# One chain of row maxima per attention head instead of four, and new numbers for the scheduler of a fused attention and MLP kernel

## The chip, the cores and the metric

The kernel runs on one core of one Trainium2 chip. A core has TensorE (PE, matrix products; its weight loads are shown apart as PEld), VectorE (DVE), ScalarE (ACT), GpSimd (POOL) and SyncE (SP, which here issues nearly all DMAs). The matmuls write to PSUM, 8 banks of 128 x 512 float32 values. The metric is the time of one execution on the device in microseconds (us), the median of several runs; lower is better.

## What is computed

The input x is 2048 x 1024 and is normalised row by row. Two branches read the result: an attention with 32 heads of width 32, and an MLP of width 3584 with the mish activation. The output is x + s * silu(mlp).

```python
qkv = (xn @ wqkv).reshape(B, S, 3, H, Dh)            # S 2048, H 32, Dh 32
scores = jnp.einsum("bhqd,bhkd->bhqk", q, k) * (Dh ** -0.5)
p = _softmax(scores, axis=-1)
o = jnp.einsum("bhqk,bhkd->bhqd", p, v)
s = o.transpose(...).reshape(B, S, D) @ wo
h = jnp.einsum("bsd,df->bsf", xn, w1) + b1           # F 3584
act = h * jnp.tanh(softplus(h))
g = _silu(jnp.einsum("bsf,fd->bsd", act, w2))
return x + s * g
```

## The kernel before

Matrix values that need full precision are split into a high and a low part (fp32r), and a product is made of three matmuls: high x high, high x low, low x high.

The work has three stages. First come the norm, the projections to q, k and v, and the splitting of the MLP's weights; their results go to DRAM. The second stage runs attention and MLP together, and its order is made by a planner (class `Plan`, L78) while the program is built. The third stage is the rest of the output projection with the gate (`op` matmuls, L1107).

In the second stage five streams offer matmuls to the planner, and every other operation is an `Op` (L67) with an engine, a duration, needs, and rings from which it takes a place (PSUM banks and SBUF tiles).

- `s_stream` (L684) makes the scores of head h a first time, only for their maxima. For each of 16 query tiles (`qt`) and 4 key chunks (`kc`) one 128 x 512 matmul `s` (L695) goes to a bank, and VectorE reduces the bank to one column of maxima (`mx`, L701).
- `m_chain` (L711) turns maxima into something that a matmul can use. Its steps: the maximum over the 4 chunks, negated (`nm`, DVE L714); high and low part (`hl`, a copy on ACT and a subtraction on POOL); a transpose on PE (`mtp`, L527); a copy to SBUF (`mt`, ACT); and two DMAs on SP's queue that write rows 96 and 97 of the head's q stack. Before, it runs once for each group of 4 query tiles, four times a head.
- `t_stream` (L761) makes the scores again, transposed, with the negated maxima already added by rows 96 and 97: for key tile T (16 a head) four matmuls `t` (L775), each followed by an exponential on ACT (`p`, L264). POOL adds up the tiles `p` into `z` (L804, one add per tile), and after 6, 5 and 5 key tiles (`GROUPS`, L32) `product` (L814) issues the matmuls `pv` (L822). `norm` (L838) makes the sums with the matmuls `zp` (L848) and divides on DVE (L859, L862, L865).
- `h_stream` (L909) and `y_stream` (L996) make the MLP: 24 matmuls `h` (L923) per tile, mish on DVE and ACT (L942 to L978), and the matmuls `y` (L1011), whose results DVE adds up in `yacc` (L1031).
- `p_stream` (L1110) begins the output projection.

The q and k stacks of a head lie in one of three pairs of SBUF tiles. `stack_load` (L681) loads the pair of head h with six DMAs of 256 KB, after the last `t` of head h-3. SP issues in the planner's order, and each DMA waits there for what it needs, so that a waiting one holds back those behind it. Weight tiles `w1` (1 MB) and `w2` (512 KB) and a head's `v` go through the same queue.

The planner goes forward in its own time. At each step it takes, for the engine that is free first, the ready operation with the smallest key. For the matmuls of the streams the key is a due time: for `s` it is that of the `t` in `LEAD` key tiles before the next head's first one. For the others it is the time at which they became ready, less `urgent`: a negative `U_MX` holds the maxima back behind others. `S_B`, `T_B` and `D_B` are the banks that `s`, `t` (with `mtp`) and the MLP (with `zp`) may hold at one time, of seven in all; `LATE` delays `mtp` and `zp` unless PE is already in the products' column mode; `Y0` is the lag of `y` behind `h`.

Of the kernel before, what the change touches and what calls it, by code (L numbers as in the profile page):

```python
# [9 lines left out]
F32 = mybir.dt.float32  # L10
F32R = mybir.dt.float32r
AF = mybir.ActivationFunctionType
ALU = mybir.AluOpType
AX = mybir.AxisListType
# [4 lines left out]
P = 128  # L19
KT = D // P  # L20
NC = S // 512
NT = S // P
# [4 lines left out]
W1_V = 20  # L27
NS = H * NT

MM, PV = 0.228, 0.86  # L30

GROUPS, YB = (6, 5, 5), 2  # L32

LEAD, LATE = 5, 4.0

PS, ACTS, W2S, Y0, Y1 = 7, 3, 5, 0.6, 0.17

AHEAD, BEHIND = 1.5, 1

S_B, T_B, D_B = 2, 2, 4  # L40

U_MX, U_Y = -2.0, 1.0


class Later:
# [32 lines left out]
class Plan:  # L78
# [7 lines left out]
    SETTLE = 0.2  # L86

    AHEAD = {"DVE": 0.08, "ACT": 0.1, "POOL": 0.0}
    SEM, SWITCH, LAND, RATE = 0.07, (0.25, 0.13), 2.0, 0.25e6

    def __init__(self):
        self.at = {"PE": 0.0, "ACT": 0.0, "DVE": 0.0, "POOL": 0.0, "SP": 0.0}
# [122 lines left out]
def body(ctx: ExitStack, tc: tile.TileContext, x, wqkv, wo, w1, b1, w2, out):  # L215
    nc = tc.nc
# [6 lines left out]
    def pool(stack, name, bufs, side="left", **kw):  # L223
        return stack.enter_context(tc.tile_pool(name=name, bufs=bufs, side=side, reuse_waits="tile", **kw))
# [41 lines left out]
    def copy(out_, in_, scale=1.0):  # L266
        nc.scalar.activation(out_, in_, AF.Copy, scale=scale)  # L267

    def move(out_, in_, eng=None):

        (eng or nc.sync).dma_start(out_.bitcast(F32), in_.bitcast(F32))

    def low(eng, out_, in_, high):

        eng.tensor_tensor(out_, in_, high.bitcast(F32), ALU.subtract)  # L275
# [137 lines left out]
    for t in range(2, NT + 2):  # L413
# [19 lines left out]
        if t > 7:  # L433
            c, k = t // 4 - 1, t % 4 * 2
# [63 lines left out]
    early = pool(att0, "early", 1, side="right")  # L498
    qst, kst = [], []
# [16 lines left out]
    hls = [early.tile([P, P], F32R, name=f"hl{i}") for i in range(2)]  # L516
# [6 lines left out]
    def parts(i):  # L523
        return hls[i][:, :8].rearrange("p (a b) -> p a b", a=2)

    def turn(tp, i):
        nc.tensor.matmul(tp[:, :P], hls[i], ident_r, start=True, stop=True)  # L527
# [141 lines left out]
    def bank(at, name):  # L669
        return ps_a.tile([P, 512], F32, tag=f"b{at['b']}", name=name)  # L670

    def op(*args, **kw):
        return plan.add(Op(*args, **kw))

    total = 2 * 4 * NS * MM + NC * FT * 48 * MM + NS * PV
    slot = total / NS


    loaded, m_there, last_t, last_pv, final, stored = {}, {}, {}, {}, {}, {}
# [5 lines left out]
    def s_stream():  # L685
        for h in range(1, H):
            while h not in loaded:
                yield None
            for g in range(4):
                maxes, tiles = [], {}  # L690
                for qt in range(4 * g, 4 * g + 4):
                    for kc in range(4):
                        def mm(at, h=h, qt=qt, kc=kc, tiles=tiles):
                            tiles[qt, kc] = sp_ = bank(at, f"s{h}_{qt}_{kc}")
                            nc.tensor.matmul(sp_, qst[h % 3][:, qt * P:(qt + 1) * P],  # L695
                                             kst[h % 3][:, kc * 512:(kc + 1) * 512], start=True, stop=True)

                        def mx(at, h=h, g=g, qt=qt, kc=kc, tiles=tiles):
                            if qt == 4 * g and kc == 0:
                                tiles["mx"] = early.tile([P, 4, 4], F32, tag=f"mx{at['mx']}", name=f"mx{h}_{g}")  # L700
                            nc.vector.reduce_max(tiles["mx"][:, qt % 4, kc:kc + 1], tiles[qt, kc], axis=AX.X)  # L701

                        m = Op("PE", MM, key=slot * (16 * (h - 1) + qt + (kc + 1) / 4 - LEAD), need=[loaded[h]],
                               emit=mm, take=["s", "b"])
                        yield m
                        maxes.append(op("DVE", 0.69, need=[m] + maxes[:1], emit=mx, give=[("s", m), ("b", m)], urgent=U_MX,
                                        take=["mx"] if qt == 4 * g and kc == 0 else []))
                m_chain(h, g, maxes, tiles)
        final["s"] = m

    def m_chain(h, g, maxes, tiles):  # L711
        def r1(at):
            tiles["nm"] = early.tile([P, 4], F32, tag=f"nm{at['nm']}", name=f"nm{h}_{g}")
            nc.vector.tensor_reduce(tiles["nm"], tiles["mx"], axis=AX.X, op=ALU.max, negate=True)  # L714

        def r2(at):
            tiles["hl"] = at["hl"]
            copy(parts(tiles["hl"])[:, 0], tiles["nm"])

        def r3(at):  # L720
            hl = parts(tiles["hl"])
            low(nc.vector if h == 0 else nc.gpsimd, hl[:, 1], tiles["nm"], hl[:, 0])

        def r4(at):
            tiles["tp"] = tp = bank(at, f"mtp{h}_{g}")
            turn(tp, tiles["hl"])

        def r5(at):
            tiles["mt"] = early.tile([8, P], F32R, tag=f"mt{at['mt']}", name=f"mt{h}_{g}")
            copy(tiles["mt"], tiles["tp"][:8, :P])  # L730

        def r6(at):
            for a in range(2):
                move(qst[h % 3][96 + a:97 + a, g * 512:(g + 1) * 512]
                     .rearrange("o (t p) -> o t p", p=P), tiles["mt"][4 * a:4 * a + 4, :])

        a = op("DVE", 0.18, need=maxes, emit=r1, take=["nm"], give=["mx"])
        a = op("ACT", 0.21, need=[a], emit=r2, take=["hl"])
        a = op("POOL" if h else "DVE", 0.25, need=[a], emit=r3, give=["nm"], key=-1)
        a = op("PE", 0.07, need=[a], emit=r4, take=["t", "b"], give=["hl"], late=LATE if h else 0.0)  # L740
        a = op("ACT", 0.28, need=[a], emit=r5, take=["mt"], give=[("t", a), ("b", a)])
        m_there[h, g] = op("SP", 0.2, need=[a], emit=r6, give=["mt"], bytes_=4096)


    exps, adds, uses = {}, {}, {}
# [415 lines left out]
    plan.take_now("mx", 1)  # L1161
    loaded[1] = None
    m_chain(0, 3, [], {"mx": negm[0]})
    plan.run([t_stream(), s_stream(), h_stream(), y_stream(), p_stream()])
    ph.close()

# [46 lines left out]
    for c in range(NC):  # L1213
        for s in range(4):
            t = 4 * c + s
            if t + 4 < NT:
                start(t + 4)
            for dh in range(2):
# [5 lines left out]
                if c:  # L1224
                    n = 2 * s + dh
# [39 lines left out]
```

## Time and profile before

| what | before |
|---|---|
| median of 3 runs | 3448.2 us |
| lowest and highest run | 3447.49 and 3449.71 us |
| profiled execution: span from first to last instruction | 3445.5 us |
| profiled execution: own total beside the span | not given |
| granted TensorE clock, mean | 1.000 |
| busy: PE, PEld, DVE, ACT, POOL | 99, 74, 68, 57, 72% of the span |
| the planned stage, first `s` of head 1 to first `op` | 578.65 to 3267.09 us |

Times in rows are in us from the span's start unless they are marked ns. A row of a group has line, engine, operation, out<-in, shapes and count, then busy us and mean ns of one, then the engine's idle time before them and what ended it. A row of the timeline has start, duration, engine, line, operation and count, and in brackets the idle time before it with its releaser. L12 is line 12 of the kernel. Matmuls overlap in these rows: one starts before the last has ended, so that a row's duration is not the time from one to the next.

### The profile page before, as it was taken

To read this page: it belongs to the slowest core of one execution; us is meant where nothing else is said; L and a number is where in the kernel's file an instruction comes from. 1 tells how busy PE (TensorE), PEld (TensorE's weight loads), DVE (VectorE), ACT (ScalarE), POOL (GpSimd) and SP (SyncE) were. 2 spreads that over 40 slices of the span, in tenths; PEclk is the share of its full clock that TensorE was granted. 3 is DMA by queue.
4 is the path that set the end of the run, shared out by engine and by line. 5 is a ranking of instruction groups with operands and counts; after the bars stand their busy time and mean duration, and the time that the engine had idled before them with its cause. 6 is when DMAs were issued, how large, how long until landed. Compare 5 with 4: busy or idle time off the path is not lost.

```text
span 3445.5 us, 48527 instructions
## 1 busy us (share of the span) xinstructions
PE 3414.9 (99%) x17920; PEld 2546.2 (74%) x17920; DVE 2341.4 (68%) x3843; ACT 1962.8 (57%) x3298; POOL 2469.8 (72%) x846
## 2 busy tenths in 40 slices
PE   8999999999999999999999999999999999999999
PEld 8998887676777767777667677677777777776787
DVE  6012236887878777787788778778877787776633
ACT  6111112666666667666666676666666666666621
POOL 0644342898888888888888888888888888888800
PEclk9999999999999999999999999999999999999999
DMA  8998896443434354343433443334345444334382
GB/s 293 299 298 303 288 319 223 112 120 99 118 105 122 105 165 134 113 117 104 123 111 111 147 144 115 111 102 119 111 122 160 135 122 122 108 103 132 119 309 86
DMA packets 294193, 529.80 MB, mean 154 GB/s; under 512 B 88810, under 2 KB 147178, under 8 KB 270186
## 3 DMA queue, kind: packets, MB, share of 16 engines
q1 hardware_dynamic: 274100, 484.74, 45.6%
q10 hardware_dynamic: 19856, 41.95, 3.4%
q8 instruction: 142, 2.33, 0.3%
q14 instruction: 95, 0.78, 0.1%
HBM read 386.89 MB, written 138.67 MB: 153 GB/s over the span
## 4 chain that ended last, share of the span: by engine, by line
PE 95%; DVE 2%; ACT 2%; issue 1%; DMA 1%; POOL 1%; SPq 0%; POOLq 0%; ACTq 0%
PE h L923 17%; PE y L1011 17%; PE pv L822 13%; PE t L775 13%; PE s L695 13%; PE qk L623 10%; PE op L1107 5%; PE v L324 5%; ACT p L264 1%; DVE mx L701 1%; PE zp L848 1%; PE s L550 0%; POOL z L804 0%; DMA qstack<-mt 0%; PE mtp L527 0%
## 5 line engine op out<-in xcount | busy, mean ns | idle before, releaser
L804 POOL TENSOR_TENSOR z<-z,p 128x2048 f32<-128x2048 f32 x448 | 2065.8, 4611 | 195.8 <-ACT p L264 173.2
L264 ACT ACTIVATE p<-t,zero 128x512 f32<-128x512 f32 x2048 | 1376.7, 689 | 625.2 <-PE t L775 615.6
L701 DVE TENSOR_REDUCE mx<-s 128x1 f32<-128x512 f32 x1984 | 1323.0, 685 | 454.1 <-PE s L695 450.4
L1011 PE MATMUL y<-w,act 128*128 128x512 f32 x2688 | 928.0, 392 | 1.0 <-DVE yacc L1031 0.8
L775 PE MATMUL t<-qstack,kstack 128*128 128x512 f32 x2048 | 799.0, 394 | 5.3 <-DMA qstack<-mt 3.0
L695 PE MATMUL s<-kstack,qstack 128*128 128x512 f32 x1984 | 777.6, 395 | 6.3 <-DVE mx L701 3.2
L923 PE MATMUL h<-xr,w 128*128 128x512 f32 x2016 | 693.9, 391 | 1.0 <-ACT p L264 1.0
L1011 PEld LDWEIGHTS y<-w,act 128*128 128x128 f32 x2688 | 502.0, 188 | 114.9 <-issue 4.2
L775 PEld LDWEIGHTS t<-qstack,kstack 128*128 128x128 f32 x2048 | 384.4, 188 | 124.7 <-issue 25.4
L695 PEld LDWEIGHTS s<-kstack,qstack 128*128 128x128 f32 x1984 | 371.3, 188 | 119.6 <-issue 18.4
L822 PE MATMUL pv<-p,v 128*32 128x512 f32 x4096 | 459.3, 594 | 0.0
L923 PEld LDWEIGHTS h<-xr,w 128*128 128x128 f32 x2016 | 376.8, 188 | 84.6 <-issue 3.4
L623 PE MATMUL qk<-xc,qkw 128*128 128x512 f32 x1536 | 350.9, 389 | 0.0
L804 POOL TENSOR_TENSOR z<-p,p 128x2048 f32<-128x2048 f32 x32 | 147.9, 4621 | 278.6 <-ACT p L264 218.7
L623 PEld LDWEIGHTS qk<-xc,qkw 128*128 128x128 f32 x1536 | 288.2, 188 | 59.8
L822 PEld LDWEIGHTS pv<-p,v 128*32 128x32 f32 x4096 | 123.3, 110 | 281.5 <-issue 281.1
L1031 DVE TENSOR_TENSOR yacc<-yacc,y 128x512 f32<-128x512 f32 x416 | 282.7, 680 | 47.4 <-PE y L1011 45.2
L923 PE MATMUL h<-xc,w 128*128 128x512 f32 x672 | 233.3, 391 | 0.4 <-DVE yacc L1031 0.4
L275 DVE TENSOR_TENSOR qst<-qk,qst 128x512 fp32r<-128x512 f32 x64 | 44.2, 691 | 246.2 <-ACT qst L267 246.2
L267 ACT ACTIVATE qst<-qk 128x512 fp32r<-128x512 f32 x64 | 38.3, 598 | 302.6 <-PE qk L623 287.4
L324 PE MATMUL v<-vw,xc 128*128 128x256 f32 x1536 | 190.8, 285 | 2.9 <-POOL vw L275 1.5
L324 PEld LDWEIGHTS v<-vw,xc 128*128 128x128 f32 x1536 | 186.6, 193 | 4.5 <-POOL vw L275 1.9
(91 smaller groups left out, 2391.2 us busy)
## 6 DMA issues: line engine op xcount, KB each, us to landing
w<-w1s SPq DMA_DIRECT2D x112, 1024.0 KB
w<-w2s SPq DMA_DIRECT2D x224, 512.0 KB
w2s<-pw SPq DMA_DIRECT2D x56, 512.0 KB
qstack<-qs SPq DMA_DIRECT2D x96, 256.0 KB
kstack<-ks SPq DMA_DIRECT2D x96, 256.0 KB
w1s<-w1p SPq DMA_DIRECT2D x20, 1024.0 KB
praw<-in_B_w_dram SPq DMA_DIRECT2D x72, 256.0 KB
x<-in_A_x_dram SPq DMA_DIRECT2D x32, 512.0 KB
```

The source lines that it names most:

```text
L264: nc.scalar.activation(out_, in_, fn, bias=zero if bias is None else bias, scale=scale)
L324: nc.tensor.matmul(ps[:, :256], xc[t // 4][:, a, k, (t % 4) * P:(t % 4 + 1) * P], w[:, b, k], start=n == 0, stop=n == 3 * KT - 1)
L623: nc.tensor.matmul(ps, w[:, a, k], xc[c][:, b, k], start=n == 0, stop=n == 3 * KT - 1)
L695: nc.tensor.matmul(sp_, qst[h % 3][:, qt * P:(qt + 1) * P], kst[h % 3][:, kc * 512:(kc + 1) * 512], start=True, stop=True)
L701: nc.vector.reduce_max(tiles["mx"][:, qt % 4, kc:kc + 1], tiles[qt, kc], axis=AX.X)
L775: nc.tensor.matmul(tp, kst[h % 3][:, kt * P:(kt + 1) * P], qst[h % 3][:, c * 512:(c + 1) * 512], start=True, stop=True)
L804: nc.gpsimd.tensor_tensor(zs[h], pts[T - 1] if kt == 1 else zs[h], pts[T], ALU.add)
L822: nc.tensor.matmul(pv[h][c * DH:(c + 1) * DH, :], vt[h][:, k, :], pts[T - kt + k][:, c * 512:(c + 1) * 512], start=k == 0, stop=k == NT - 1)
L923: nc.tensor.matmul(t["h"], w1t[n][:, a, k], xts_[c][:, b, k], start=i == 0, stop=i == 3 * KT - 1)
L1011: nc.tensor.matmul(t["y"], acts[n][:, p, s * P:(s + 1) * P], w2t[m_][:, q], start=j == 0 and i == 0, stop=j == YB - 1 and i == 2)
L1031: nc.vector.tensor_tensor(ya, ya, t["y"], ALU.add)
L1107: nc.tensor.matmul(ps[t, dh], ohl[t // 4, k][:, a, s * P:(s + 1) * P], wt[k][:, b, r], start=k == 0 and i == 0, stop=k == KT - 1 and i == 2)
```

## The change

There are two parts. `s_stream` no longer makes groups: the maxima of a whole head go to one tile of 16 x 4 columns, and `m_chain` runs once a head with n = 16 query tiles. Its tiles have 16 and 32 columns or rows instead of 4 and 8, and its two DMAs write 2048 columns instead of 512. The part of head 0 that the planner does still runs with n = 4. Head h's first `t` now needs the only chain of its head, so the maxima of all 16 query tiles.

The other part is the table of numbers for the planner.

```diff
-MM, PV = 0.228, 0.86
+MM, PV = 0.22667, 0.8587
-LEAD, LATE = 5, 4.0
-
-PS, ACTS, W2S, Y0, Y1 = 7, 3, 5, 0.6, 0.17
+LEAD, LATE = 15, 3.0
+
+PS, ACTS, W2S, Y0, Y1 = 7, 3, 5, 1.2, 0.17
-S_B, T_B, D_B = 2, 2, 4
-
-U_MX, U_Y = -2.0, 1.0
+S_B, T_B, D_B = 2, 2, 5
+
+U_MX, U_Y = 0.0, 1.0
...
-    SEM, SWITCH, LAND, RATE = 0.07, (0.25, 0.13), 2.0, 0.25e6
+    SEM, SWITCH, LAND, RATE = 0.07, (0.2, 0.125), 2.0, 0.25e6
...
-            for g in range(4):
-                maxes, tiles = [], {}
-                for qt in range(4 * g, 4 * g + 4):
-                    for kc in range(4):
+            maxes, tiles = [], {}
+            for qt in range(NT):
+                for kc in range(4):
...
-                m_chain(h, g, maxes, tiles)
+            m_chain(h, 0, maxes, tiles, NT)
...
-    def m_chain(h, g, maxes, tiles):
+    def m_chain(h, g, maxes, tiles, n=4):
+        kind = "mh" if n == NT else "m"
+
+        def hl_parts():
+            return hls[tiles["hl"]][:, :2 * n].rearrange("p (a b) -> p a b", a=2)
...
-            tiles["mt"] = early.tile([8, P], F32R, tag=f"mt{at['mt']}", name=f"mt{h}_{g}")
-            copy(tiles["mt"], tiles["tp"][:8, :P])
+            tiles["mt"] = early.tile([2 * n, P], F32R, tag=f"{kind}t{at['mt']}", name=f"mt{h}_{g}")
+            copy(tiles["mt"], tiles["tp"][:2 * n, :P])
...
-        a = op("PE", 0.07, need=[a], emit=r4, take=["t", "b"], give=["hl"], late=LATE if h else 0.0)
+        a = op("PE", 0.12, need=[a], emit=r4, take=["t", "b"], give=["hl"], late=LATE if h else 0.0)
...
-        m_there[h, g] = op("SP", 0.2, need=[a], emit=r6, give=["mt"], bytes_=4096)
+        a = op("SP", 0.2, need=[a], emit=r6, give=["mt"], bytes_=1024 * n)
+        for c in range(g, g + n // 4):
+            m_there[h, c] = a
```

The order changes everywhere in the second stage. Three places show how. In the names, s14_0_1 is head 14, query tile 0, chunk 1; t193_2 is key tile 193 (head 12, its second), chunk 2; pv11, zp11, mtp13 and v12 are of heads 11, 13 and 12; h41 is MLP tile 41.

The first place is PE at the end of head 11's product and its sum. The rows of before:

```order
L923 MATMUL h41_15128<-xr1_12055,w1_41_14917 128x512
L822 MATMUL pv11_14754<-p187_15001,v11_14408 32x512 x4
L822 MATMUL pv11_14754<-p188_15063,v11_14408 32x512 x4
L822 MATMUL pv11_14754<-p189_15109,v11_14408 32x512 x4
L822 MATMUL pv11_14754<-p190_15148,v11_14408 32x512 x4
L822 MATMUL pv11_14754<-p191_15198,v11_14408 32x512 x4
L848 MATMUL zp11_15350<-z11_14561,ones_159 32x512 x4
L1011 MATMUL y19_1_3_15316<-w2_78_14723,act38_14779 128x512
L775 MATMUL t193_3_15360<-qstack0_2719,kstack0_2720 128x512
L695 MATMUL s13_6_3_15362<-kstack1_2726,qstack1_2725 128x512
L923 MATMUL h41_15128<-xr1_12055,w1_41_14917 128x512
```

And now:

```order
L1017 MATMUL y19_1_0_15012<-w2_79_14752,act39_14754 128x512
L828 MATMUL pv11_14479<-p187_14715,v11_14132 32x512 x4
L828 MATMUL pv11_14479<-p188_14779,v11_14132 32x512 x4
L828 MATMUL pv11_14479<-p189_14810,v11_14132 32x512 x4
L828 MATMUL pv11_14479<-p190_14850,v11_14132 32x512 x4
L828 MATMUL pv11_14479<-p191_14901,v11_14132 32x512 x4
L854 MATMUL zp11_15047<-z11_14287,ones_159 32x512 x4
L694 MATMUL s14_0_0_15056<-kstack2_5385,qstack2_5384 128x512
L694 MATMUL s14_0_1_15062<-kstack2_5385,qstack2_5384 128x512
L527 MATMUL mtp13_0_15064<-ident_r_166,hl1_2728 128x128
L929 MATMUL h41_14819<-xr1_11818,w1_41_14619 128x512
```

Before, the scores of head 13 were under way at this place (query tile 6); now those of head 14 begin here, with the stack (kstack2, qstack2) that head 11 has just left, and head 13's only transpose stands behind them.

The second place is SP around the load of head 14's stack. The rows of before:

```order
L271 DMA w1_42_15122<-w1s14_96 128x2048
L271 DMA w2_81_15182<-w2s13_123 128x2x512
L271 DMA w2_82_15194<-w2s12_122 128x2x512
L752 DMA v12_15229<-vs1_79 128x16x32
L271 DMA qstack2_5384<-zeros_153 2x2048
L271 DMA qstack2_5384<-qs3_65 32x2048
L271 DMA kstack2_5385<-ks3_73 32x2048
...
L271 DMA qstack1_2725<-mt13_0_15320 1x4x128 x2
L271 DMA w2_83_15371<-w2s13_123 128x2x512
L271 DMA w2_84_15390<-w2s14_124 128x2x512
```

And now:

```order
L271 DMA w2_80_14767<-w2s12_122 128x2x512
L271 DMA w1_42_14823<-w1s14_96 128x2048
L758 DMA v12_14923<-vs1_79 128x16x32
L271 DMA qstack2_5384<-zeros_153 2x2048
L271 DMA qstack2_5384<-qs3_65 32x2048
L271 DMA kstack2_5385<-ks3_73 32x2048
...
L271 DMA w2_81_14999<-w2s13_123 128x2x512
L271 DMA w2_82_15016<-w2s12_122 128x2x512
L271 DMA w1_43_15072<-w1s15_97 128x2048
L271 DMA qstack1_2725<-mt13_0_15078 1x16x128 x2
```

The load stands at the same place of the queue, behind a weight tile and v; what has moved is its first user, from some 60 us behind it to the place shown on PE. The maxima of head 13 now go in one pair of DMAs.

The third place is VectorE at the division of head 7 (zp7, o7). The rows of before:

```order
L942 TENSOR_SCALAR e27_12062<-h27_11794,bias1_154 128x512
L859 TENSOR_TENSOR zp7_12037<-zp7_12037,rz7_12045 128x512
L701 TENSOR_REDUCE mx9_1_11907<-s9_6_2_12053 128x1
L862 SCALAR_TENSOR_TENSOR zp7_12037<-zp7_12037,rz7_12045 128x512
L952 SCALAR_TENSOR_TENSOR h27_11794<-h27_11794,bias1_154,e27_12062 128x512
L701 TENSOR_REDUCE mx9_1_11907<-s9_6_3_12064 128x1
L865 SCALAR_TENSOR_TENSOR o7_12042<-zp7_12037,o7_12042 128x512
L959 SCALAR_TENSOR_TENSOR h27_11794<-e27_12062,h27_11794 128x512
L701 TENSOR_REDUCE mx9_1_11907<-s9_7_0_12084 128x1
```

And now:

```order
L865 TENSOR_TENSOR zp7_11871<-zp7_11871,rz7_11885 128x512
L1037 TENSOR_TENSOR yacc_5386<-yacc_5386,y12_1_1_11830 128x512
L700 TENSOR_REDUCE mx9_11167<-s9_15_3_11900 128x1
L868 SCALAR_TENSOR_TENSOR zp7_11871<-zp7_11871,rz7_11885 128x512
L700 TENSOR_REDUCE mx10_11925<-s10_0_0_11904 128x1
L718 TENSOR_REDUCE nm9_0_11930<-mx9_11167 128x16
L871 SCALAR_TENSOR_TENSOR o7_11877<-zp7_11871,o7_11877 128x512
L700 TENSOR_REDUCE mx10_11925<-s10_0_1_11923 128x1
```

Before, two elementwise rows of the division and the MLP stand between one maximum and the next; now one row of the division alternates with a maximum here.

More of the change, by code (lines that the diff above doesn't have):

```diff
@@ L688, in s_stream @@
                 yield None
-            for g in range(4):
-                maxes, tiles = [], {}
-                for qt in range(4 * g, 4 * g + 4):
-                    for kc in range(4):
[L693 to L707, printed above, removed]
-                m_chain(h, g, maxes, tiles)
@@ new lines, in s_stream, with mm, mx @@
+            maxes, tiles = [], {}
+            for qt in range(NT):
+                for kc in range(4):
+                    def mm(at, h=h, qt=qt, kc=kc, tiles=tiles):
+                        tiles[qt, kc] = sp_ = bank(at, f"s{h}_{qt}_{kc}")
+                        nc.tensor.matmul(sp_, qst[h % 3][:, qt * P:(qt + 1) * P],
+                                         kst[h % 3][:, kc * 512:(kc + 1) * 512], start=True, stop=True)
+                    def mx(at, h=h, qt=qt, kc=kc, tiles=tiles):
+                        if qt == 0 and kc == 0:
+                            tiles["mx"] = early.tile([P, NT, 4], F32, tag=f"mxh{at['mx']}", name=f"mx{h}")
+                        nc.vector.reduce_max(tiles["mx"][:, qt, kc:kc + 1], tiles[qt, kc], axis=AX.X)
+                    m = Op("PE", MM, key=slot * (16 * (h - 1) + qt + (kc + 1) / 4 - LEAD), need=[loaded[h]],
+                           emit=mm, take=["s", "b"])
+                    yield m
+                    maxes.append(op("DVE", 0.69, need=[m] + maxes[:1], emit=mx, give=[("s", m), ("b", m)], urgent=U_MX,
+                                    take=["mx"] if qt == 0 and kc == 0 else []))
@@ L709, in s_stream @@
+            m_chain(h, 0, maxes, tiles, NT)
         final["s"] = m
-    def m_chain(h, g, maxes, tiles):
+    def m_chain(h, g, maxes, tiles, n=4):
+        kind = "mh" if n == NT else "m"
+        def hl_parts():
+            return hls[tiles["hl"]][:, :2 * n].rearrange("p (a b) -> p a b", a=2)
         def r1(at):
-            tiles["nm"] = early.tile([P, 4], F32, tag=f"nm{at['nm']}", name=f"nm{h}_{g}")
+            tiles["nm"] = early.tile([P, n], F32, tag=f"n{kind}{at['nm']}", name=f"nm{h}_{g}")
@@ L717, in r2 @@
             tiles["hl"] = at["hl"]
-            copy(parts(tiles["hl"])[:, 0], tiles["nm"])
+            copy(hl_parts()[:, 0], tiles["nm"])
         def r3(at):
-            hl = parts(tiles["hl"])
+            hl = hl_parts()
             low(nc.vector if h == 0 else nc.gpsimd, hl[:, 1], tiles["nm"], hl[:, 0])
@@ L728, in r5 @@
         def r5(at):
-            tiles["mt"] = early.tile([8, P], F32R, tag=f"mt{at['mt']}", name=f"mt{h}_{g}")
-            copy(tiles["mt"], tiles["tp"][:8, :P])
+            tiles["mt"] = early.tile([2 * n, P], F32R, tag=f"{kind}t{at['mt']}", name=f"mt{h}_{g}")
+            copy(tiles["mt"], tiles["tp"][:2 * n, :P])
         def r6(at):
             for a in range(2):
-                move(qst[h % 3][96 + a:97 + a, g * 512:(g + 1) * 512]
-                     .rearrange("o (t p) -> o t p", p=P), tiles["mt"][4 * a:4 * a + 4, :])
+                move(qst[h % 3][96 + a:97 + a, g * 512:g * 512 + n * P]
+                     .rearrange("o (t p) -> o t p", p=P), tiles["mt"][n * a:n * a + n, :])
         a = op("DVE", 0.18, need=maxes, emit=r1, take=["nm"], give=["mx"])
```

## The prediction, made before the changed kernel was run

> **What bounds the kernel now.** I read the page's engine table first, then the chain that ended last, then the costliest groups. Rows, in this order: the engine table, four pieces of the chain (start, us, what), the first matmul of the stage that the change touches, and the groups of TensorE (count, busy us, mean ns, idle before).
>
> ```profile
> PE 3414.9 (99%) x17920; PEld 2546.2 (74%) x17920; DVE 2341.4 (68%) x3843; ACT 1962.8 (57%) x3298; POOL 2469.8 (72%) x846
> 482.02 5.44 PE qk L623 x24
> 1444.54 5.29 PE pv L822 x48
> 3267.09 174.09 PE op L1107 x768
> 578.65 0.49 PE L695 MATMUL s<-kstack,qstack 128*128 128x512 f32 x1 [1.12 <-ACT mt L267]
> L1011 PE MATMUL y<-w,act 128*128 128x512 f32 x2688 | 928.0, 392 | 1.0 <-DVE yacc L1031 0.8
> L775 PE MATMUL t<-qstack,kstack 128*128 128x512 f32 x2048 | 799.0, 394 | 5.3 <-DMA qstack<-mt 3.0 <-ACT p L264 1.6
> L695 PE MATMUL s<-kstack,qstack 128*128 128x512 f32 x1984 | 777.6, 395 | 6.3 <-DVE mx L701 3.2 <-ACT mt L267 1.1 <-DVE mx L554 1.1
> L923 PE MATMUL h<-xr,w 128*128 128x512 f32 x2016 | 693.9, 391 | 1.0 <-ACT p L264 1.0
> L923 PE MATMUL h<-xc,w 128*128 128x512 f32 x672 | 233.3, 391 | 0.4 <-DVE yacc L1031 0.4
> L822 PE MATMUL pv<-p,v 128*32 128x512 f32 x4096 | 459.3, 594 | 0.0
> ```
>
> TensorE is the bound. Its matmuls overlap (mean 392 ns, but one starts every 174.09/768 = 0.2267 us in the output projection), so the idle column hides waits: a wait shows as a start later than 0.2267 us after the last. I therefore take the planned stage, 578.65 to 3267.09 = 2688.4 us, and subtract its work. The next rows give the small prices, as start times: a transpose among full matmuls, the step into a product, the sum's matmuls behind it, and the count of transposes.
>
> ```profile
> 1437.67 0.39 PE L923 MATMUL h<-xr,w 128*128 128x512 f32 x1
> 1437.89 0.22 PE L527 MATMUL mtp<-ident_r,hl 128*128 128x128 f32 x1
> 1437.95 0.45 PE L1011 MATMUL y<-w,act 128*128 128x512 f32 x1
> 1438.24 0.39 PE L695 MATMUL s<-kstack,qstack 128*128 128x512 f32 x1
> 1444.15 0.39 PE L1011 MATMUL y<-w,act 128*128 128x512 f32 x1
> 1444.47 1.92 PE L822 MATMUL pv<-p,v 128*32 128x512 f32 x16
> 1505.84 1.04 PE L848 MATMUL zp<-z,ones 128*32 128x512 f32 x8
> 1506.81 0.50 PE L775 MATMUL t<-qstack,kstack 128*128 128x512 f32 x1
> L527 PE MATMUL mtp<-ident_r,hl x128: 218/220/328, 551.7 to 3155.7; 128*128 128x128 f32 x128
> ```
>
> Work: 9408 matmuls of 512 columns (2688+2048+1984+2016+672) x 0.2267 = 2132.6; products 4096 x 5.29/48 = 451.4; 96 steps into a product x (0.32-0.23) = 9; 32 sums x 0.97 = 31; 125 transposes. One transpose takes 1438.24-1437.67 = 0.57 less two steps of 0.227, so 0.117 us: half shows before the next matmul (0.06), half behind it (0.29 for 0.23). 125 x 0.117 = 14.6. In all 2638.6, and **about 50 us are waits**.
>
> **What the waits are.** The largest inside the stage: first the PE rows, then the VectorE rows of the same place.
>
> ```profile
> 1255.89 0.50 PE L695 MATMUL s<-kstack,qstack 128*128 128x512 f32 x1
> 1257.74 0.49 PE L695 MATMUL s<-kstack,qstack 128*128 128x512 f32 x1 [1.35 <-DVE mx L701]
> 1255.16 0.68 DVE L701 TENSOR_REDUCE mx<-s 128x1 f32<-128x512 f32 x1
> 1255.76 0.69 DVE L862 SCALAR_TENSOR_TENSOR zp<-zp,rz 128x512 f32<-128x512 f32 x1
> 1256.35 0.75 DVE L952 SCALAR_TENSOR_TENSOR h<-h,bias,e 128x512 f32<-128x512 f32 x1
> 1257.01 0.68 DVE L701 TENSOR_REDUCE mx<-s 128x1 f32<-128x512 f32 x1
> 666.05 0.47 PE L775 MATMUL t<-qstack,kstack 128*128 128x512 f32 x1 [2.37 <-DMA qstack<-mt]
> ```
>
> A score matmul waits for its bank (1.85 us instead of 0.23), since VectorE put two elementwise steps between two maxima. The last row is another kind: head 1's negated maxima land late.
>
> **The change, part by part.**
>
> *Transposes.* 93 of 124 go: 93 x 0.117 = **10.9 us gained** on the bounding engine. Nothing hides these, so nothing gives them back. The 31 left have the same 128x128 shape. The other steps of a chain (a small reduction, two copies, a subtraction, two DMAs) go 93 times too, but on engines at 57 to 72%: counted as nothing. The reduction that now reads 128x64 has no row; whatever it costs, between the small ones and the 0.68 of a 128x512 one, it runs 31 times on VectorE, 55 us or more ahead of its user for heads 9 to 31. SP is rid of 186 small DMAs that wait on a copy of ScalarE with weight tiles queued behind them; those tiles aren't waited for in the rows above, so that is nothing either.
>
> *Bank waits.* The scheduler's own numbers change (real durations, maxima no longer held back, one bank more for MLP tiles), so the order changes everywhere. In the orders I laid PE's rows end to end with the prices above and looked at each PSUM bank: how long from the last matmul into it until the first of its next tile. Under 1.5 us (a 0.39 us matmul, an evacuation of 0.68 and what else is queued hardly fit) there are 154 reuses before and 78 after: s 24 to 14, t 74 to 38, y 21 to 11, transposes 35 to 15. On VectorE the stretches of exactly three or four elementwise rows between two maxima fall from 75 to 23 (longer ones: 19 and 22). Of the 50 us I take 35 as bank waits; the rest is the stage's opening, head 1 and jitter. That is a choice. 35 x 76/154 = **17 us gained**, between 0 (the waits move to other places) and 50 (all gone).
>
> *The stack's load.* Scores run up to 15 slots ahead instead of 5. A head's q and k stack (six DMAs, 1.5 MB) can be loaded only when the head three before has done its last t matmul. Before, the first s stood 57 to 65 us behind that t; now it stands 12.2 to 15.1 us behind for most of heads 11 to 31 (head 14: 43 matmuls x 0.2267 + 5 key tiles of the product, 40 instructions x 0.110, + 0.97 = 15.1; heads 20 and 31: 12.2; head 29: 40 x 0.2267 = 9.1). So the load, which had 45 us of cover, has almost none. Rows of a quick load, then of a slow one: last t, the issues, and the windows (us, busy by engine, granted clock, DMA share, GB/s) where the traffic ends.
>
> ```profile
> 1576.53 0.39 PE L775 MATMUL t<-qstack,kstack 128*128 128x512 f32 x1
> 1576.95 0.51 SPq L271 DMA_DIRECT2D qstack<-zeros  x1
> 1580.38 0.42 SPq L271 DMA_DIRECT2D kstack<-ks  x1
> 1584.00:1586.00 2.00, 2.00 (x12) 1.21 (x14) 2.00 (x4) 1.17 (x3) 0.98 (x1) 1.00 0.98 213
> 1586.00:1588.00 2.00, 2.00 (x24) 0.65 (x20) 0.24 (x1) 0.00 (x0) 0.00 (x0) 1.00 0.14 31
> 2996.50 2.10 SPq L271 DMA_DIRECT2D w<-w2s  x2
> 2998.76 0.48 SPq L271 DMA_DIRECT2D w<-w1s  x1
> 2999.30 0.52 SPq L752 DMA_DIRECT2D v<-vs  x1
> 3000.16 0.39 PE L775 MATMUL t<-qstack,kstack 128*128 128x512 f32 x1
> 3000.58 4.90 SPq L271 DMA_DIRECT2D qstack<-zeros  x1
> 3014.00:3016.00 2.00, 2.00 (x11) 1.63 (x9) 1.90 (x4) 2.00 (x5) 0.00 (x0) 1.00 0.92 197
> 3016.00:3018.00 2.00, 2.00 (x10) 1.69 (x9) 2.00 (x4) 1.71 (x4) 1.84 (x1) 1.00 0.17 27
> ```
>
> The quick load's traffic ends about 10 us after its t, the slow one's about 16.5, with 2 MB of weights and a v tile just ahead of it in the queue. In the new order of SP a weight tile whose buffer comes free less than 4 us before that t stands ahead of the load for about a dozen heads; 0.5 MB at the 213 GB/s of the fourth of these rows is 2.5 us more than the quick case, so 12.5 to 13.5 against 12.2 to 14.5. I take 0.75 us x 12 = **9 us lost**, between 0 and, if all 23 heads are as the slow one, 23 x 2.7 = 62. In the order the first s stands right behind the product and the sum in most heads, and TensorE works in order: whatever is late there stops everything.
>
> [...]
>
> *Head 1's maxima.* They stand behind a stack load in SP's queue before and after, so the 2.37 us at 666 stay: nothing.
>
> Sum: -10.9 - 17 + 9 = -18.9 on the span of 3445.5, which is 3426.6; the span lies 2.7 under the median of 3448.2 (the profiled execution's own total isn't given apart from it), so **3429**.
>
> **The rivals.**
>
> *Only the transposes count.* The bank waits move instead of falling, or the loads eat what they give: 0 to 11 us, 3437 to 3448. For it: each evacuating engine still serves its queue in order, and reuses under 1.7 us rise (s 144 to 206, t 372 to 478). Against: the halved count above.
>
> *The loads come late (slower).* Price 2.7 us x 23 heads = 62 - 28 = +34, 3482. It decides against the change once the loads are 28/23 = 1.2 us late on average. For it: the slow load above. Against: most first s stand behind the product, and the slow load had 2 MB ahead, and most have one tile or none.
>
> *The clock goes too.* If such waits also halved TensorE's clock for as long as they lasted, 5 us of waiting and 5 at half speed (2.5 lost) a head would cost 23 x 7.5 = 173, less 28: 3593. Against it, the clock of 1.00 around the wait of 2.37 us:
>
> ```profile
> 664.00:670.00 6.00, 3.94 (x27) 1.91 (x31) 3.33 (x7) 2.86 (x5) 0.79 (x2) 1.00 1.02 353
> ```
>
> [...]
>
> *Nearly all waits go:* 11 + 40 = 51 us, 3397.
>
> **How the numbers follow.** Forecast (8 to 30 us gained) 0.71; only the transposes 0.13; loads late 0.07; clock 0.01; nearly all waits gone 0.08. 0.2%, 6.9 us, is about what a measurement can tell from no change. Faster: 0.71 + 0.08 + 0.04 of the transposes' 0.13 = 0.83; same 0.09; slower 0.08. The range runs from a good part of the last rival, 3407 (41 us), to the near end of the first, 3447.
>
> **What would show it.** Right: 35 transposes; the stage 17 to 20 us shorter; fewer PE starts held by a max or an exponential; a few waits of under 2 us at the first s of a head. Wrong: first s waiting 3 us or more at most heads (loads), or as many waits at t, h and y as before (only the transposes). A stage that shortens by 40 us would say that I priced the loads too high or the bank waits too low.

## The result: slower by half a per cent, against the forecast

| what | before | after |
|---|---|---|
| median | 3447.97 us | 3465.59 us |
| lowest and highest run | 3447.49 and 3449.71 | 3461.81 and 3468.02 |
| profiled execution: span | 3445.5 | 3464.0 |
| granted clock, mean | 1.000 | 0.999 |
| planned stage | 2688.4 | 2702.0 |

The ratio after to before is 1.0049, with a 95% interval of 1.0035 to 1.0064. The forecast was 3429. The lines of the profile after that answer to those shown of before are, first, the engine table of the page:

```profile
PE 3434.3 (99%) x17827; PEld 2539.6 (73%) x17827; DVE 2324.8 (67%) x3750; ACT 1945.7 (56%) x3112; POOL 2467.2 (71%) x753
```

VectorE, ScalarE and GpSimd lost their 93 small steps each (two each on ScalarE), and TensorE lost 93 matmuls, as the change says. Yet its busy time rose from 3414.9 to 3434.3. The chain by time (start, us, what) and the first matmul of the stage:

```profile
482.22 5.45 PE qk L623 x24
...
3281.14 178.14 PE op L1113 x768
```

```profile
579.16 0.50 PE L694 MATMUL s<-kstack,qstack 128*128 128x512 f32 x1 [1.12 <-ACT mt L267]
```

The stage lasts 3281.14 - 579.16 = 2702.0 us, 13.5 more than before (3267.09 - 578.65). The output projection behind it, which the change does not touch at all, takes 178.14 us for the same 768 matmuls that took 174.09: 4.05 more. The projections ahead of the stage (`qk`) are as they were. The groups of TensorE (count, busy us, mean ns, idle before):

```profile
L1017 PE MATMUL y<-w,act 128*128 128x512 f32 x2688 | 936.7, 394 | 1.2 <-DVE yacc L1037 0.5 <-ACT p L264 0.4
L781 PE MATMUL t<-qstack,kstack 128*128 128x512 f32 x2048 | 795.5, 394 | 3.0 <-DMA qstack<-mt 1.7 <-ACT p L264 1.0
L694 PE MATMUL s<-kstack,qstack 128*128 128x512 f32 x1984 | 777.1, 397 | 8.2 <-issue 2.7 <-DMA qstack<-qs 1.5 <-ACT mt L267 1.1
L929 PE MATMUL h<-xr,w 128*128 128x512 f32 x2016 | 705.3, 394 | 1.4 <-DMA xr<-xs 1.3
L828 PE MATMUL pv<-p,v 128*32 128x512 f32 x4096 | 459.3, 594 | 0.0
...
L527 PE MATMUL mtp<-ident_r,hl 128*128 128x128 f32 x35 | 10.0, 289 | 0.0
```

The 35 transposes are there, and the idle column is small. What stands out is the mean of one: 394 ns for `h` where it was 391, and for `y` where it was 392, in groups that wait for next to nothing. The products `pv` are unchanged to the tenth. The longest waits of TensorE (us in total, times, longest):

```profile
PE s L694 <- issue: 2.7, 4, 1.1
PE t L781 <- DMA qstack<-mt: 1.7, 1, 1.7
...
PE s L694 <- DMA qstack<-qs: 1.5, 1, 1.5
...
PE t L781 <- ACT p L264: 1.0, 3, 0.5
...
PE s L694 <- DVE mx L700: 0.7, 2, 0.5
```

So neither of the signs that I had named for "wrong" shows: the first `s` of a head does not wait 3 us, and matmuls are held less by maxima (0.7 us at `s`, 3.2 before) and exponentials (1.0 at `t`, 1.6 before). The idle time ahead of `s` rose from 6.3 to 8.2 us, but that of all these groups together is what it was (13.8 us, 14.0 before), and the stage grew by 13.5. The matmuls themselves come at a slower pace, at a granted clock of 1.00. Here are 100 us of the output projection, before and then after (busy time and count by engine from PE on, then clock, DMA share, GB/s): 443 matmuls fall into the first, 433 into the second.

```profile
3300.00:3400.00 100.00, 100.00 (x443) 82.82 (x442) 43.94 (x66) 23.69 (x32) 0.00 (x0) 1.00 0.62 220
```

```profile
3300.00:3400.00 100.00, 100.00 (x433) 80.81 (x432) 42.78 (x64) 26.46 (x35) 0.00 (x0) 1.00 0.70 252
```

**Theories.** *Place:* the chain's new tiles (two of 16 x 4 maxima at 256 bytes a partition, two `nm` at 64, one `mt` at 512: 1152 bytes in all) are taken from the pool in which the q and k stacks lie, and push all three pairs 1152 bytes down. Taken modulo 256, the stacks' start in a partition goes from 192 (byte 194752, for instance) to 64 (193600), while x, `w1`, `w2`, `act` and the products' `p` and `v` stay at 192. (Two smaller operands are elsewhere in both kernels: the sum's `ones` at 64, and the slices of `v`, 128 bytes apart, at 192 and 64 in turn.) Six of the eight tiles `wo` of the output projection take over the stacks' places and move with them; the other two lie in places of `w1`, at 192. *Order:* the new order itself slows the stream, by contention or by waits too short to show. *Clock:* the clock is lower than the records say. Place says that the time goes with the addresses and not with the order; Order says the reverse.

### The profile page after: what moved, and what is told of

It is laid out like the page before. It is cut to its first block, busy times and chain, and to the rows that moved or that the text cites. A ratio compares the mean times of both kernels' runs of the same rounds, so it can differ in the third digit from the quotient of the medians.

```text
span 3464.0 us, 47242 instructions
## 1 busy us (share of the span) xinstructions
PE 3434.3 (99%) x17827; PEld 2539.6 (73%) x17827; DVE 2324.8 (67%) x3750; ACT 1945.7 (56%) x3112; POOL 2467.2 (71%) x753
## 4 chain that ended last, share of the span: by engine, by line
PE 97%; DMA 1%; DVE 1%; ACT 1%; issue 0%; POOL 0%; SPq 0%; POOLq 0%; ACTq 0%
PE h L929 18%; PE y L1017 17%; PE t L781 13%; PE s L694 13%; PE pv L828 13%; PE qk L623 10%; PE op L1113 5%; PE v L324 5%; PE zp L854 1%; PE s L550 0%; PE pt L379 0%; DVE mx L700 0%; DMA xr<-xs 0%; ACT p L264 0%; DMA qstack<-mt 0%
## 5 line engine op out<-in xcount | busy, mean ns | idle before, releaser
L929 PE MATMUL h<-xr,w 128*128 128x512 f32 x2016 | 705.3, 394 | 1.4 <-DMA xr<-xs 1.3
L828 PE MATMUL pv<-p,v 128*32 128x512 f32 x4096 | 459.3, 594 | 0.0
L275 DVE TENSOR_TENSOR qst<-qk,qst 128x512 fp32r<-128x512 f32 x64 | 44.2, 691 | 249.4 <-ACT qst L267 249.4
```

What stands on the lines that cost most here:

```text
L828: nc.tensor.matmul(pv[h][c * DH:(c + 1) * DH, :], vt[h][:, k, :], pts[T - kt + k][:, c * 512:(c + 1) * 512], start=k == 0, stop=k == NT - 1)
L929: nc.tensor.matmul(t["h"], w1t[n][:, a, k], xts_[c][:, b, k], start=i == 0, stop=i == 3 * KT - 1)
```

## The experiments

All of these do the whole of the computation. The filler tiles named below are never read; the two kernels had `pad` and `pad2` already.

**The stacks put back.** The kernel after, with a filler tile 128 bytes larger, so that the stacks start at 192 modulo 256 again.

```diff
-    nc.vector.memset(early.tile([P, 16], F32, name="pad2"), 0.0)
+    nc.vector.memset(early.tile([P, 48], F32, name="pad2"), 0.0)
```

> The changed kernel with the small filler tile ahead of the stacks 128 B a partition longer, so that the q and k stacks lie at 193472 instead of 193600, which is 192 instead of 64 modulo 256, as all other operands of the stage and as the stacks before the change. Order and instructions are the same. Theory P (place): the spacing of full matmuls goes back from 231 to 227 ns in the stage and from 232 to 227 in the output projection; 32 + 4 us less, 3427 to 3431. Rival O (order): the new order itself makes matmuls slower; nothing changes, 3462 to 3468. Rival C (clock): the granted clock of 0.999 stands for a slower PE; nothing changes either.

3428.16 us (3426.69 to 3430.08), ratio to before 0.9942 (0.9927 to 0.9957). Its first matmul of the stage and its piece of the chain:

```profile
578.75 0.49 PE L694 MATMUL s<-kstack,qstack 128*128 128x512 f32 x1 [1.12 <-ACT mt L267]
```

```profile
3247.63 174.09 PE op L1113 x768
```

The stage is 2668.9 us, the projection 174.09 as before. One filler's 128 bytes, with the same table of numbers, are worth 3465.59 - 3428.16 = 37.4 us. Its span of 3426.5 is the 3426.6 of the forecast's sum; that they meet to 0.1 us is luck, as the terms below show.

**The stacks of the kernel before put off.** The same edit in the kernel before, whose order and chains stay.

> The kernel before with the same 128 B added, so that its stacks lie at 64 instead of 192 modulo 256; order and instructions are those of before. Theory P: the spacing rises from 227 to 231 and 232, about 36 us more, 3480 to 3488. Rivals O and C: no change, 3448.

3484.59 us (3483.46 to 3486.76), ratio 1.0106 (1.0091 to 1.0121): 37.0 us slower than the kernel before, measured beside it (3447.58).

```profile
3299.16 178.14 PE op L1107 x768
```

The projection has the 178.14 of the kernel after, to the hundredth. Order falls: the slow pace comes without the change, and the change without the slow pace.

**Moved by 256, and by 64.** The kernel after with `pad2` 256 bytes larger (another address, the same remainder 64), and 64 bytes larger (remainder 0).

```diff
-    nc.vector.memset(early.tile([P, 16], F32, name="pad2"), 0.0)
+    nc.vector.memset(early.tile([P, 80], F32, name="pad2"), 0.0)
...
-    nc.vector.memset(early.tile([P, 16], F32, name="pad2"), 0.0)
+    nc.vector.memset(early.tile([P, 32], F32, name="pad2"), 0.0)
```

> The changed kernel with 256 B added instead of 128: the stacks move, but stay at 64 modulo 256. Theory P with the remainder by 256 as what counts: as the changed kernel, 3462 to 3468 and 231 ns. If it is the absolute place, or a longer period than 256 B, the spacing changes here; by rivals O and C, as the changed kernel.

> The changed kernel with 64 B added: the stacks lie at 0 modulo 256, 64 away from the others' 192. Theory P, where any difference of remainders costs the same: 231 ns, 3462 to 3468. Where the cost grows with the distance: between 3430 and 3465. Where only a difference of 128 costs: 227 ns and 3427 to 3431. Rivals O and C: 3462 to 3468.

3466.81 us (ratio 1.0052, 1.0036 to 1.0069) and 3466.38 (1.0052, 1.0037 to 1.0067). The first is the kernel after again, so that the address counts by its remainder, as far as one shift by 256 can show it. The second shows that remainder 0 is no better than 64, where the others are at 192; its projection is a little faster:

```profile
3283.53 176.68 PE op L1113 x768
```

**All operands off together.** The kernel before with 128 bytes of filler on both sides of the memory, so that the operands of `s`, `t`, `h`, `y`, `pv` and `op` all start at 64.

```diff
+    nc.vector.memset(consts.tile([P, 32], F32, name="pad3"), 0.0)
...
-    pad = pool(ctx, "pad", 1, side="right").tile([P, 8], F32, name="pad")
+    pad = pool(ctx, "pad", 1, side="right").tile([P, 40], F32, name="pad")
```

> The kernel before with 128 B of filler at both ends of the memory, so that all operands of TensorE, stacks, weights, activations and x alike, lie at 64 instead of 192 modulo 256. If what counts is that consecutive matmuls and weight loads read at the same remainder (relative): 227 ns and 3448. If 192 itself is the good remainder (absolute): 231 ns or more in every stage, 3485 or above.

3447.73 us, ratio 1.0 (0.9991 to 1.0009).

```profile
3269.01 174.09 PE op L1108 x768
```

Nothing is wrong with 64. What costs is that operands differ.

**The MLP's operands off.** The kernel before with the filler first in the MLP's pool: `w2` and `act` go to 64, and `p`, `v` and `z` behind them; the stacks, x and `w1` stay at 192.

```diff
+    nc.vector.memset(mlp.tile([P, 32], F32, name="pad3"), 0.0)
```

> The kernel before with 128 B of filler ahead of the MLP's tiles alone: w2 and act (operands of y) lie at 64 modulo 256, stacks, w1 and x at 192. By the relative theory the spacing rises wherever a y stands beside an h, s or t, but h among h, s and t stays at 227, and the output projection, none of whose operands moved, stays at 227: 3460 to 3475. If only the stacks' place matters: 3448.

3475.94 us, ratio 1.008 (1.0063 to 1.0096).

```profile
3295.66 174.10 PE op L1108 x768
```

It costs 28 us with the stacks untouched, just more than expected, and the projection, whose operands all lie at 192 here, is as fast as before. In this kernel each of the full matmuls has both its operands at one remainder (`y` at 64; `s`, `t` and `h` at 192). So a matmul need not be mixed within itself: it is enough that the next ones lie elsewhere.

**Off by 32.** The kernel after with `pad2` 96 bytes larger: the stacks at 224, 32 bytes off the others.

```diff
-    nc.vector.memset(early.tile([P, 16], F32, name="pad2"), 0.0)
+    nc.vector.memset(early.tile([P, 40], F32, name="pad2"), 0.0)
```

> The kernel after with the filler tile pad2 at [P, 40], 96 bytes more, so that the q and k stacks lie 32 bytes off the other operands of TensorE modulo 256 (remainder 224 against 192), where offsets of 64 and of 128 have cost 37 to 38 us and an offset of 0 nothing. If any difference of the remainders costs, the time is 3460 to 3470 and the output projection takes 176 to 178.2 us for its 768 matmuls. If what counts is only the remainder in steps of 64 bytes (operands in the same 64 bytes, or the same place to the nearest 64), the time is 3425 to 3432 and the projection 174.1. A time between, 3435 to 3455, would say that a smaller offset costs in proportion. I expect the first, with the chance of two in three.

3477.01 us, ratio 1.0083 (1.0066 to 1.01), more than I expected.

```profile
3294.42 178.79 PE op L1113 x768
```

An offset of 32 costs 48.9 us against the stacks at 192, more than 64 (38.2) and 128 (37.4). Smaller offsets weren't tried.

**The parts one by one.** First the new numbers alone, in the kernel before, with its four chains a head (the stacks stay at 192); then the one chain alone, with the old numbers and the stacks put back. Of the two edits, a few lines each:

```diff
-LEAD, LATE = 5, 4.0
+LEAD, LATE = 15, 3.0
...
-U_MX, U_Y = -2.0, 1.0
+U_MX, U_Y = 0.0, 1.0
```

```diff
-LEAD, LATE = 15, 3.0
+LEAD, LATE = 5, 4.0
...
-    nc.vector.memset(early.tile([P, 16], F32, name="pad2"), 0.0)
+    nc.vector.memset(early.tile([P, 48], F32, name="pad2"), 0.0)
```

> The kernel before with the scheduler's new numbers alone: four chains a head, stacks at 192 modulo 256 as before, so no part of the slower matmuls. Counted in its order: 128 transposes, bank reuses under 1.5 us 127 (before 154, changed kernel 78), first s 12 to 18 us behind the last t for heads 11 to 31. If the numbers cut waits by themselves, as the prediction had it for the two parts together: 3436 to 3444 (waits down about 12, loads 7 lost). If only the transposes counted: 3448 to 3455.

> The changed kernel with the scheduler's old numbers: one chain a head and nothing else, stacks put back to 192 modulo 256. Counted: 35 transposes, reuses under 1.5 us 100, first s 57 to 64 us behind the last t. Transposes alone: 93 x 0.117 = 11 less than before, 3437. If waits at banks fall with the fewer chain steps too: 3430 to 3435. If the chain's removal gave nothing and all came from the numbers: 3448.

3441.04 us (3436.26 to 3445.5), ratio 0.9978 (0.9968 to 0.9988); and 3430.69 (3430.08 to 3431.08), ratio 0.9947 (0.9933 to 0.9962). Against 3448.37, measured beside them, the numbers alone gain 7.3 us (4 to 11 by the interval) and the chain alone 17.7; both together, with the stacks put back, gained 19.4 on the kernel before measured beside them. So, with a lead of 15, the numbers add at most about 2 to the chain, which the intervals can't tell from nothing.

**The lead.** The kernel after with the stacks put back, and scores at most 12 key tiles ahead, or 9, instead of 15.

```diff
-LEAD, LATE = 15, 3.0
+LEAD, LATE = 12, 3.0
```

> The changed kernel with the place put back (as the first experiment) and LEAD 12 instead of 15, so that the first s stands 22 to 27 us behind the last t and the stack's load has its cover again. If the waits at the first s of a head (about 7 us in the first experiment's trace) are what the loads cost: they go, 3420 to 3423. If they only move to other places: 3427 to 3431.

> The changed kernel with the place put back and LEAD 9. If the 13 us that LEAD 12 gave over 15 are the cover of the stack's load, cover beyond the load's landing gives nothing more: 3411 to 3418. If fewer due scores ahead are better as such: 3405 to 3411. If the early scores (15) were good for something else that is lost with less lead: 3420 or above.

3414.8 us (3413.72 to 3415.73), ratio 0.9901 (0.9884 to 0.9917); and 3414.92 (3414.03 to 3415.63), ratio 0.9904 (0.989 to 0.9919). These beat both kernels, by 33.6 us against the one before measured beside the first, and LEAD 12 lies below the 3420 to 3423 expected. What LEAD 15 cost shows in the `s` group and the waits: first LEAD 15 with the stacks put back, group and longest wait, then the group at LEAD 12.

```profile
L694 PE MATMUL s<-kstack,qstack 128*128 128x512 f32 x1984 | 772.1, 395 | 10.0 <-issue 5.7 <-ACT mt L267 1.1 <-DVE mx L554 1.1
```

```profile
PE s L694 <- issue: 5.7, 6, 1.7
```

```profile
L694 PE MATMUL s<-kstack,qstack 128*128 128x512 f32 x1984 | 774.2, 393 | 3.3 <-ACT mt L267 1.1 <-DVE mx L554 1.1 <-DVE mx L700 1.1
```

The 10.0 us of idle time ahead of `s` become 3.3: the six waits of "issue", up to 1.7 us each, are gone. In the kernel after one such wait has its releaser named, at the first `s` of head 20:

```profile
2103.90 1.04 PE L854 MATMUL zp<-z,ones 128*32 128x512 f32 x8
2104.87 0.33 PE L527 MATMUL mtp<-ident_r,hl 128*128 128x128 f32 x1
2106.70 0.47 PE L694 MATMUL s<-kstack,qstack 128*128 128x512 f32 x1 [1.50 <-DMA qstack<-qs]
```

It stands behind the sum and a transpose and waits for the stack. The forecast had counted heads 20, 29 and 31 as those with the least cover, and all three wait. At 9 nothing more is gained than at 12.

**The maxima held back.** The kernel after with the stacks put back and `U_MX` as it was before.

```diff
-U_MX, U_Y = 0.0, 1.0
+U_MX, U_Y = -2.0, 1.0
```

> The changed kernel with the place put back and U_MX at -2.0 as before, so that maxima are held back behind elementwise work. If serving the maxima at once is what took the waits at s away: 3431 to 3437. If the banks' reuse alone decides (72 under 1.5 us against 78): 3426 to 3430.

3426.33 us (3425.27 to 3432.16), against 3428.16 (3426.69 to 3430.08): no difference that can be told.

## Why the prediction was wrong

**The step that failed** is the one ahead of all terms: I "laid PE's rows end to end with the prices above", that is, I let a matmul of 512 columns keep its 0.2267 us in the changed kernel. In the sum this is the term of 9408 x 0.2267 = 2132.6 us, and outside the stage the projection's 174.09, both taken over as they were. That price was read from the trace of before, in which both operands of every such matmul of the stage and the projection lie at one remainder. The change's new tiles move the stacks, and the price goes with it; no term, no bound and no rival asked where tiles lie. The diff had it in plain sight: tiles of 16 x 4 and of 32 rows instead of 4 x 4 and 8, in the pool of the stacks.

How much, by the sum: in the trace of the kernel after, the 9297 steps from one full matmul (`s`, `t`, `h`, `y`) to the next full one take 2177.4 us from start to start. In the kernel with the stacks put back, whose numbers for the planner are the same, the same 9297 take 2142.3. That is 35.1 us, 3.8 ns a step. The stage as a whole differs by 33.1 (2702.0 and 2668.9), since the steps out of transposes and inside products are some 2 us shorter in the slower kernel; the projection's 4.05 comes on top. By addresses alone the runs differ by 37.4 (after) and 37.0 (before).

The kernel after shows the cause within itself, near the end of the stage, where `t` and `y` mix at first and `y` runs alone behind that:

```profile
3257.39 0.39 PE L781 MATMUL t<-qstack,kstack 128*128 128x512 f32 x1
3257.62 1.09 PE L1017 MATMUL y<-w,act 128*128 128x512 f32 x4
3258.55 0.39 PE L781 MATMUL t<-qstack,kstack 128*128 128x512 f32 x1
3258.78 0.62 PE L1017 MATMUL y<-w,act 128*128 128x512 f32 x2
3259.24 0.40 PE L781 MATMUL t<-qstack,kstack 128*128 128x512 f32 x1
3259.47 0.86 PE L1017 MATMUL y<-w,act 128*128 128x512 f32 x3
3260.18 0.39 PE L781 MATMUL t<-qstack,kstack 128*128 128x512 f32 x1
3260.41 0.62 PE L1017 MATMUL y<-w,act 128*128 128x512 f32 x2
3260.87 0.39 PE L781 MATMUL t<-qstack,kstack 128*128 128x512 f32 x1
3261.10 10.63 PE L1017 MATMUL y<-w,act 128*128 128x512 f32 x46
3271.66 4.50 PE L828 MATMUL pv<-p,v 128*32 128x512 f32 x40
```

And the same place with the stacks put back:

```profile
3224.68 0.62 PE L1017 MATMUL y<-w,act 128*128 128x512 f32 x2
3225.14 0.39 PE L781 MATMUL t<-qstack,kstack 128*128 128x512 f32 x1
3225.36 0.62 PE L1017 MATMUL y<-w,act 128*128 128x512 f32 x2
3225.82 0.39 PE L781 MATMUL t<-qstack,kstack 128*128 128x512 f32 x1
3226.05 0.84 PE L1017 MATMUL y<-w,act 128*128 128x512 f32 x3
3226.72 0.39 PE L781 MATMUL t<-qstack,kstack 128*128 128x512 f32 x1
3226.95 0.62 PE L1017 MATMUL y<-w,act 128*128 128x512 f32 x2
3227.41 0.39 PE L781 MATMUL t<-qstack,kstack 128*128 128x512 f32 x1
3227.63 10.59 PE L1017 MATMUL y<-w,act 128*128 128x512 f32 x46
3238.15 4.50 PE L828 MATMUL pv<-p,v 128*32 128x512 f32 x40
```

Mixed, 16 matmuls take 3261.10 - 3257.39 = 3.71 us, 232 ns each, against 3227.63 - 3224.68 = 2.95 for 13, 227 each. The 46 `y` alone, whose operands are all at 192, take 10.56 and 10.52 us up to the product, nearly the same. The cost also lingers. I sorted the steps under 260 ns that lead from one `h` or `y` to another, in the kernel after, by their number in an unbroken row of `h` and `y` since the last `s` or `t`: the first ones take 231.8 ns in the mean (1545 of them), the fourth 229.5 (62), the twelfth and later 226.7 (53). With the stacks put back the same three take 227.2, 226.7 and 226.7.

**The terms that I did name** come out near their sizes with the stacks put back, not all of them for the reason given.

- *Transposes*, 10.9: 35 are left, and the sum below closes to half a microsecond with the price of 0.117. The reduction without a row takes 214 ns, as cheap as thought:

```profile
L718 DVE TENSOR_REDUCE nm<-mx 128x16 f32<-128x64 f32 x31 | 6.6, 214 | 1.4
```

- *Bank waits*, 17: the steps between full matmuls hold 2141.5 - 9202 x 0.227 = 52.6 us of excess before and 2142.3 - 9297 x 0.227 = 31.9 with the stacks put back. The fall of 20.7 contains the half of each transpose's price that shows behind it (93 x 0.06 = 5.6), which leaves 15.1. The size is near, but the way to it was not borne out, so that luck has a part in it. I scaled the waits with the number of banks reused in under 1.5 us. With the transposes' half taken off (7.4 us with four chains a head, 1.9 with one), the excess is 45 us at 154 such reuses (before), 24 at 127 (numbers alone: 2129.1 us for 9243 steps), 42 at 100 (chain alone: 2151.9 for 9285) and 30 at 78 (both): it does not follow the count. Holding the maxima back again changes nothing either, so the shorter stretches between maxima on VectorE do not come from that number, or don't matter.
- *The loads*, 9: the steps from a transpose into a full matmul, where 13 of the first `s` of heads 4 to 31 stand, take 11.5 us at LEAD 15 and 4.6 at LEAD 12, so 6.9 of waits. -10.9 - 15.1 + 6.9 = -19.1, and the stage is 2688.4 - 2668.9 = 19.5 shorter. Two more waits for stacks, 2.0 us at the first `s` of heads 19 and 29, stand behind an `h` and so lie within the 15.1. Counted at the first `s` itself the loads cost about 8 us, against the 9 of the forecast.
- *The whole price of LEAD 15* was larger than its loads: LEAD 12 gains 13.4. The steps between full matmuls fall by a further 5.8 there (2142.3 to 2136.5), of which 2.0 are the waits of heads 19 and 29; why the order at LEAD 12 leaves fewer other waits isn't settled.
- *Head 1's maxima* still come late (a wait of 2.00 us with the stacks put back, where it was 2.37), as said.

**The parts don't add.** I booked the bank waits to the numbers and only the transposes to the chain. The numbers alone gained 7.3, near the 8 that their two terms make. The chain alone gained 17.7, and the numbers add some 2 at most on top of it with a lead of 15. What the chain gains beyond its transposes I can't divide: the excess of the steps between full matmuls falls by 8.4 in that run (52.6 to 44.2), of which 5.6 are the transposes' own.

**The rivals.** The loads come late, but by 8 us and not 62. The clock was not it: it is 0.999 in the mean, the pace stays slow at a clock of 1.00, and the run off by 32 had a mean of 1.000. No run shows half speed for as long as a wait lasts, from which that rival's 173 us were worked out in part; each of the two kernels has one stretch of 3.41 us at half clock in the stage. What the chances lacked was a rival in which the bounding engine's own price changes.

## What to carry to other kernels

The price of an instruction can belong to its operands' places as well as to its shape (a matmul of one shape every 226.7 ns here, or every 230 to 233): where a change adds or resizes a tile, work out which other tiles move, and keep all operands of the bounding engine's matmuls at one remainder of the partition address (modulo 256 bytes in these runs). When order, counts and clock agree and the pace doesn't, put the addresses back with a filler of some bytes before looking for a wait. A lead needs to be long enough for what it feeds; a longer one can eat the cover of the load that it needs itself, as 15 did here against 12 and 9 (3428.2 us against 3414.8 and 3414.9).

## What the runs showed of the hardware

**The pace and the place.** TensorE's matmuls of 128 x 512 in this kernel start every 226.7 ns where all operands, moving ones and weights, have the same remainder modulo 256 bytes in the partition, and some 230 to 233 ns apart in the mean where remainders differ by 32, 64 or 128 (the projection's 768 in 174.09 us, and in 176.68 to 178.79, 230 to 232.8 each). The products `pv` kept their 459.3 us in the kernel after; as the slices of `v` lie at two remainders in every kernel, this doesn't tell whether they would gain from one.

The projection of the kernel after tells more of the cause. Its weights, the attention's output, lie at 192 throughout, and its moving operand `wo` at 64 for six of the eight k. In a stretch of 96 matmuls (k 4 to 7, starts from 3303.11 to 3325.27 us) every moving operand is at 64 and all weights are at 192, and the starts are 233.3 ns apart from its first half to its last; with the stacks put back the same stretch has 226.7. From the fifth query tile on, k 3 with both at 192 stands between such matmuls, and the steps out of its three are 226.7 in the mean. So it takes no step from one moving operand to another place: moving rows at one remainder and weights at another are enough. The MLP's run, where each matmul has both its operands at one remainder and the time is 28 us longer, shows that the step from one matmul to the next at another remainder is enough too. What in the chip makes either slower, no run shows. Why 32 costs more than 64 and 128 is open.

**The clock.** A short stretch at half clock follows some idle times of 1.1 to 2.4 us and not others. In the kernel after, at the opening of the stage, behind two idle times of 1.1 us with one matmul between, windows with the busy time by engine, the granted clock, the DMA share and GB/s:

```profile
578.00:582.00 4.00, 1.78 (x6) 1.22 (x6) 3.96 (x9) 0.82 (x4) 0.00 (x0) 0.93 0.35 133
582.00:586.00 4.00, 4.00 (x13) 3.14 (x12) 1.81 (x4) 1.54 (x4) 0.00 (x0) 0.64 0.89 209
```

And in the kernel before, after the idle 1.35 us at 1257.74 that the prediction shows:

```profile
1256.00:1262.00 6.00, 4.45 (x11) 2.30 (x10) 6.00 (x11) 5.55 (x10) 5.56 (x2) 0.72 1.02 370
```

The clock is 0.64 in the second window of the kernel after, and 0.72 in that of the kernel before, while the wait of 2.37 us at 666 in the kernel before left it at 1.00, and so did the idle times of 1.12 and 1.11 us at the opening of its stage. With the stacks put back, the wait of 2.00 us that ends at 666.62 comes with a clock of 0.88 from 664 to 668 and 0.69 from 668 to 672. So the trace of before holds a stretch at half clock too, and the wait at 666, which the prediction set against its clock rival, is one of those without. In the traces' clock records each such stretch lasts 3.41 or 3.42 us at 0.5 (3.413 in both kernels), which costs up to 1.7 us (an estimate: half of it); there are none in the run off by 64, whose mean clock is 1.000, and three in that with all operands off, where it is 0.998. Part of the spread goes with the clock in one kernel and not in another: with the stacks put back, the execution at a mean clock of 1.000 took 3426.69 us and the one at 0.998 took 3430.08, but with the stacks off by 32 the slowest, 3479.91, had 1.000.
